# A grouped 1x1 convolution: TensorE in a loop over a 288-column input ring, a separate output ring, and a balancing piece for 15 DMA engines

## The chip, the cores and the metric

The kernel runs on one core of one Trainium2 chip. The metric is the device time in microseconds (us); the lower the better. All runs that are compared here were fast.

Names: PE is TensorE, PEld its weight loads, ACT is ScalarE, DVE is VectorE, POOL is GpSimd, SP is SyncE. Sixteen DMA engines move the data: SP issues the loads, ACT the stores.

## The reference, cut to what matters

```python
x: (1, 512, 512, 192) bf16        # 262,144 pixels of 192 channels
w: (1, 1, 4, 48, 48) bf16         # 4 groups of 48 channels, a 1x1 kernel
xg = x.reshape(1, 512, 512, 4, 48)
out = einsum('bhwgc,gcd->bhwgd', xg, w[0, 0])      # then back to (1, 512, 512, 192)
```

Each pixel is multiplied by a block-diagonal matrix. 100.7 MB are read and 100.7 MB written. In the kernel before, the DMA packets take 474 us of each DMA engine on average and the matmuls and transposes 431 us of PE, in a span of 483 us.

## The kernel before

Pixels are laid out as 128 rows by 2,048 columns, 384 bytes each. A *piece* of 104 columns is one load. Four columns are a *group*: PE transposes them (6 transposes), DVE copies a pair of groups out of PSUM, PE multiplies (6 matmuls), ACT copies the result out of PSUM. In the kernel before, ACT writes the result over the input, in the same ring, and the store leaves from there; a slot of the ring is loaded again when its store has landed. The lines below are cut and shortened; `wq.wait` waits for a semaphore.

```python
BIG = 104
RCOLS = 5 * BIG                      # one ring, 520 columns, for input and output
HEAD = (8, 20, 32)
NARROW = ((0, 16), (32, 16))         # 32 rows x 48 columns: the odd pixels, in the middle
...
        def _(sp):
            for p in pieces:
                for q in pieces:
                    if q.slot == p.slot - RCOLS // BIG:
                        wq.wait(st_sem[q.i], st_val[q])          # the store has landed
                for dram, sbuf in transfers(xf, ring, p):
                    sp.dma_start(sbuf, dram).then_inc(ld_sem[p.i], 16)
...
            for pair in range(NP):                               # PE, all written out
                if pair + 1 < NP:
                    transposes(pair + 1)
                matmuls(pair)
...
            for g in range(NG):                                  # ACT
                wq.wait(mm_done, g + 1)
                act.copy(dst_in_ring, o_ps[...]).then_inc(fa_done, 1)
                while todo and todo[0][3] <= g:
                    store()
```

## Time and profile before

| | before |
|---|---|
| time, median of 3 runs | 485.43 us (485.34 to 485.75) |
| span of the profile | 483.3 us |
| last PE instruction ends | 461.0 us |
| all DMA packets, summed, over 16 engines | 474.0 us |
| instruction-fetch packets | 50 |

The page of the kernel before. The first rows are busy times and the share of the span; then the busy tenths and the granted clock in 40 slices, then the DMA queues (q1 the loads, q10 the stores, q8 the instruction fetches) with packets, MB and their share of 16 engines' span; then the chain of waits that ended last, by engine.

```profile
PE 431.3 (89%) x6262; PEld 392.1 (81%) x6262; DVE 250.2 (52%) x262; ACT 392.6 (81%) x522; POOL 1.3 (0%) x8
...
PE   5699999999999999998599999979998999999910
...
PEclk9979999999999999999799999998999999999965
DMA  8999999999999999999999999999999999999993
...
q10 hardware_dynamic: 4360, 100.67, 48.7%
q1 hardware_dynamic: 3416, 100.68, 48.7%
q8 instruction: 50, 0.82, 0.6%
...
PE 54%; DMA 39%; ACT 1%; issue 1%; SPq 0%; ACTq 0%
```

The DMA row is full from the second slice to the last but one, while PE is done before the last slices. So the DMA engines hardly ever waited for compute here. The waits (who waited for whom: total us, times, longest) and the queue waits of SP say the same: PE's only sizeable waits are for loads, SP's are for stores to land.

```profile
ACT ring L260 <- PE o_ps L218: 61.0, 133, 7.9
PEld o_ps L218 <- ACT ring L260: 30.2, 126, 0.2
PE xT_ps L203 <- DMA ring<-in_x_dram: 21.1, 8, 6.8
```

```profile
SPq L175 <- DMA out_dram<-ring: 342.7, 15, 31.6
```

The windows view of the end (start:end, then busy us of each engine; the last three columns are granted clock, DMA share and GB/s) shows stores alone from 464 us on, until the last one lands:

```profile
452.00:464.00 12.00, 8.56 (x121) 7.24 (x118) 4.39 (x5) 9.23 (x13) 0.00 (x0) 0.95 1.00 424
464.00:476.00 12.00, 0.00 (x0) 0.00 (x0) 0.00 (x0) 0.00 (x0) 0.00 (x0) 0.50 0.81 343
476.00:488.00 12.00, 0.00 (x0) 0.00 (x0) 0.00 (x0) 0.00 (x0) 0.00 (x0) 0.61 0.09 37
```

The falling share in the last two rows is the DMA engines ending one after another. The trace's packet records do not name their engine, but on a busy engine each packet begins 3 or 4 ns before the recorded end of the one ahead of it, which lets them be chained into 16 engines. One of the 16 takes 1531 ns on average for a 39,936-byte packet for which most take 1476. It ends last, at 482.4 us. This document calls it the slow engine. The eight engines that carry instruction fetches (5 or 6 of the 50 packets each) are others.

### The profile page before, as it was taken

The page shows a single profiled execution, that of the slowest core. Times are in us where ns is not written, and L with a number is a line of the kernel's source. Part 1 is how long each engine was busy: PE and PEld are TensorE (multiplying, and loading weights), DVE is VectorE, ACT ScalarE, POOL GpSimd, SP SyncE. Part 2 cuts the span into 40 slices and gives each one's busy share as a digit, 9 for nine tenths or more (in the row PEclk, how much of TensorE's full clock was granted, in tenths as well). Part 3 has the DMA queues.
Part 4 walks back from the last instruction along what each step waited for, and adds up shares of the span by engine and source line. Part 5 has one row for each costly group of instructions (what it writes and reads, how often), then busy time and mean ns, then how long its engine had stood idle before and what let it go on. Part 6 is the DMA issues. An engine that isn't in the chain of part 4 may idle for free.

```text
span 483.3 us, 13933 instructions
## 1 busy us (share of the span) xinstructions
PE 431.3 (89%) x6262; PEld 392.1 (81%) x6262; DVE 250.2 (52%) x262; ACT 392.6 (81%) x522; POOL 1.3 (0%) x8
## 2 busy tenths in 40 slices
PE   5699999999999999998599999979998999999910
PEld 5599888898898889887588988969787898899800
DVE  2345655656555565564256555544554655556500
ACT  2669999999999999998299999877888999999920
POOL 1000000000000000000000000000000000000000
PEclk9979999999999999999799999998999999999965
DMA  8999999999999999999999999999999999999993
GB/s 351 431 406 421 449 425 421 422 424 442 434 428 419 425 420 439 425 434 424 431 434 437 424 431 428 432 431 426 434 428 428 430 424 422 439 416 427 429 390 156
DMA packets 7834, 202.23 MB, mean 418 GB/s; under 512 B 1056, under 2 KB 1056, under 8 KB 1696
## 3 DMA queue, kind: packets, MB, share of 16 engines
q10 hardware_dynamic: 4360, 100.67, 48.7%
q1 hardware_dynamic: 3416, 100.68, 48.7%
q8 instruction: 50, 0.82, 0.6%
q14 instruction: 8, 0.07, 0.0%
HBM read 100.68 MB, written 100.66 MB: 417 GB/s over the span
## 4 chain that ended last, share of the span: by engine, by line
PE 54%; DMA 39%; ACT 1%; issue 1%; SPq 0%; ACTq 0%
PE o_ps L218 31%; PE xT_ps L203 22%; DMA ring<-in_x_dram 20%; DMA out_dram<-ring 19%; ACT ring L260 1%; SPq L175 0%; ACTq L254 0%; SPq L169 0%
## 5 line engine op out<-in xcount | busy, mean ns | idle before, releaser
L260 ACT CAST ring<-o_ps 128x768 bf16<-128x768 f32 x521 | 391.3, 802 | 68.5 <-PE o_ps L218 61.0
L242 DVE COPY xT_sb<-xT_ps 128x1536 bf16<-128x1536 bf16 (+1 forms) x261 | 249.6, 956 | 206.0 <-PE xT_ps L203 206.0
L218 PE MATMUL o_ps<-wt,xT_sb 128*128 128x144 bf16 (+1 forms) x3126 | 292.0, 236 | 5.9 <-ACT ring L260 1.3
L218 PEld LDWEIGHTS o_ps<-wt,xT_sb 128*128 128x128 bf16 x3126 | 212.0, 99 | 43.4 <-ACT ring L260 30.2
L203 PE MATMUL xT_ps<-ident,ring 128*128 128x128 bf16 x3126 | 222.7, 221 | 21.1 <-DMA ring<-in_x_dram 21.1
L203 PEld LDWEIGHTS xT_ps<-ident,ring 128*128 128x128 bf16 x3126 | 191.1, 99 | 22.7 <-DMA ring<-in_x_dram 19.8
L188 PE MATMUL o_ps<-w_sb,esel 48*128 48x48 bf16 x10 | 0.6, 210 | 2.7 <-DMA w_sb<-in_w_dram 2.7
L188 PEld LDWEIGHTS o_ps<-w_sb,esel 48*128 48x128 bf16 x10 | 0.5, 113 | 2.6 <-POOL esel L158 2.6
L236 DVE CAST wt<-o_ps 128x480 bf16<-128x480 f32 x1 | 0.7, 658 | 3.3 <-PE o_ps L188 3.3
L260 ACT ACT_TABLE_LOAD x1 | 1.3, 1283 | 0.8 <-PEq L280 0.8
L158 POOL TENSOR_SCALAR_AFFINE_SELECT esel<-esel 48x272 bf16<-48x272 bf16 x1 | 0.4, 405 | 0.0
L155 POOL MEMSET esel<- 48x272 bf16 x1 | 0.3, 318 | 0.3 <-POOLq L280 0.3
L162 POOL TENSOR_SCALAR_AFFINE_SELECT ident<-ident 128x128 bf16<-128x128 bf16 x1 | 0.3, 285 | 0.0
L156 POOL MEMSET ident<- 128x128 bf16 x1 | 0.2, 198 | 0.0
L280 POOL MEMSET const-bfloat16-1.0<- 128x1 bf16 x1 | 0.1, 102 | 0.0
L280 POOL MEMSET const-uint8-127<- 128x1 uint8 x1 | 0.1, 102 | 0.0
L280 POOL MEMSET const-float32-0.0<- 128x1 f32 x1 | 0.1, 98 | 0.3 <-issue 0.3
L280 POOL MEMSET const-float32-1.0<- 128x1 f32 x1 | 0.1, 98 | 0.0
## 6 DMA issues: line engine op xcount, KB each, us to landing
ring<-in_x_dram SPq DMA_DIRECT2D x19, 4992.0 KB, 37.5
out_dram<-ring ACTq DMA_DIRECT2D x13, 4992.0 KB, 45.5
out_dram<-ring ACTq DMA_DIRECT2D x10, 2496.0 KB, 47.7
out_dram<-ring ACTq DMA_DIRECT2D x3, 1536.0 KB, 19.7
ring<-in_x_dram SPq DMA_DIRECT2D x1, 1536.0 KB, 8.4
out_dram<-ring ACTq DMA_DIRECT2D x1, 1152.0 KB, 16.6
ring<-in_x_dram SPq DMA_DIRECT2D x1, 960.0 KB, 5.2
out_dram<-ring ACTq DMA_DIRECT2D x1, 960.0 KB, 28.6
```

Of the source, the lines that this page charges most:

```text
L155: gp.memset(esel[:], 1.0).then_inc(p0_sem, 1)
L156: gp.memset(ident[:], 1.0).then_inc(p1_sem, 1)
L158: gp.affine_select(out=esel[:], in_=esel[:], pattern=[[-1, ECOLS]], compare_op=AluOpType.is_equal, fill=0.0, base=ESHIFT, channel_multipli ...
L162: gp.affine_select(out=ident[:], in_=ident[:], pattern=[[-1, 128]], compare_op=AluOpType.is_equal, fill=0.0, base=0, channel_multiplier=1) ...
L188: last = pe.matmul(o_ps[:, NOB - 1, col:col + CG], lhsT=esel[:, s0:s0 + 128], rhs=w_sb[:, g, :], start=True, stop=True, skip_group_check=True)
L203: last = pe.transpose(xT_ps[:, g % NXP, j * 128:(j + 1) * 128], xg[:, j * 128:(j + 1) * 128], ident[:])
L218: last = pe.matmul(o_ps[:, v % NOB, c0_:c1_], lhsT=xs[:, j * 128:(j + 1) * 128], rhs=wt[:, WOFF[tc]:WOFF[tc] + (c1_ - c0_)], start=(tc == ...
L236: dve.tensor_copy(wt[:], o_ps[:, NOB - 1, 0:WCOLS]).then_inc(wc_sem, 1)
L242: dve.tensor_copy(xT_sb[pair % NXS][:, 0:n * 2 * UC].rearrange("p (g c) -> p g c", g=n), xT_ps[:, b0:b0 + n, 0:2 * UC]).then_inc(e_done, 1)
L260: act.copy(dst, o_ps[:, v % NOB:v % NOB + 2, 0:UC]).then_inc(fa_done, 1)
L280: nc = _bacc.Bacc("TRN2", target_bir_lowering=False, num_devices=1)
```

## The change

The intent, as far as the code shows it: relieve the slow DMA engine of 64 columns, rid the others of most instruction fetches by letting PE run the same code six times, and free an input slot as soon as PE has transposed it, with a ring of its own for the output. The loop's body is written with fixed ring addresses, so it covers the input ring exactly once: 288 columns are 72 groups, 1,728 weight loads and matmuls.

```diff
-BIG = 104
-RCOLS = 5 * BIG
-HEAD = (8, 20, 32)
-NARROW = ((0, 16), (32, 16))
-NARROW_COLS = 48
+BIG = 96
+SLOTS = 3
+RCOLS = SLOTS * BIG
+OCOLS = 232
+HEAD = (8, 24, 64)
+PARTIAL = (
+    ("sync", 0, 16, 4), ("sync", 32, 16, 4),
+    ("pool", 52, 44, 11), ("pool", 20, 12, 3), ("pool", 96, 32, 8),
+)
+PARTIAL_COLS = 64
+PARTIAL_SLOT = 20
... in plan_pieces:
+    few = PARTIAL_COLS * sum(b[2] for b in PARTIAL)
+    partial = npix >= few + 128 * BIG * (PARTIAL_SLOT + 1)
... SP: a slot is free when it has been transposed
+                if freed(p) > seen:
+                    seen = freed(p)
+                    sp.wait_ge(t_done, seen)
... PE: counters are taken down again, so that the code can be repeated
+                            if j == 2 and g >= 2:
+                                last.then_inc(fa_done[(g - 2) % (2 * NTOK)], -1)
...
-            for pair in range(NP):
-                if pair + 1 < NP:
-                    transposes(pair + 1)
-                matmuls(pair)
+            first = LA // 2 if LR > 1 else NP
+            for pair in range(first):
+                step(pair)
+            if LR > 1:
+                with pe.Fori(0, LR):
+                    for pair in range(first, first + LB // 2):
+                        step(pair)
+                for pair in range(first + LR * LB // 2, NP):
+                    step(pair)
... ACT: before it writes to the out ring, the store that held those columns must have landed
+                if over[g] is not None:
+                    landed(over[g])
+                act.copy(out_columns(g)..., o_ps[...]).then_inc(fa_done[...], 1)
... gpsimd issues its share of the 64-column piece (cut)
```

More of the change, by code (lines that the diff above doesn't have):

```diff
@@ L23 @@
 ECOLS = 272
-BIG = 104
-RCOLS = 5 * BIG
-HEAD = (8, 20, 32)
-LATE = 6
-LATE_PARTS = (52, 52)
-LAST_PARTS = (32, 32, 24, 16)
-FULL = ((0, 128),)
-NARROW = ((0, 16), (32, 16))
-NARROW_COLS = 48
-NARROW_AT = (9,)
+BIG = 96
[3 more added lines that the diff above has]
+HEAD = (8, 24, 64)
+LATE_COLS = 240
+LATE_PART = 48
+LAST_PARTS = (24, 20, 16, 8)
 NXP = 4
@@ L37 @@
 NOB = 4
-class Waiter:
-    def __init__(self, eng):
-        self.eng = eng
-        self.seen = {}
-    def wait(self, sem, val):
-        if val <= 0 or self.seen.get(sem.num, 0) >= val:
-            return
-        self.seen[sem.num] = val
-        self.eng.wait_ge(sem, val)
+NTOK = 6
+FULL = (("sync", 0, 128, 128),)
+PARTIAL = (
[4 more added lines that the diff above has]
+PARTIAL_SLOT = 20
+FILL_ROWS = 5
+FILL_BEFORE = (2, 3)
 class Piece:
@@ L59, in __init__ @@
         self.blocks = []
-        for (r0, rows) in blocks:
-            self.blocks.append((r0, rows, pix))
+        for (queue, r0, rows, outer) in blocks:
+            self.blocks.append((queue, r0, rows, outer, pix))
             pix += rows * size
@@ L64, in __init__ @@
         assert size % 4 == 0 and self.at + size <= RCOLS
+class Store:
+    def __init__(self, piece, c0, c1, at):
+        self.piece, self.c0, self.c1, self.at = piece, c0, c1, at
+        self.g0, self.g1 = piece.g0 + c0 // 4, piece.g0 + c1 // 4
 def plan_pieces(npix):
-    few = NARROW_COLS * sum(rows for _, rows in NARROW)
-    at = [i for i in NARROW_AT if npix >= len(NARROW_AT) * few + 128 * (sum(HEAD) + BIG * (i + 2))]
-    cols = (npix - few * len(at)) // 128
+    few = PARTIAL_COLS * sum(b[2] for b in PARTIAL)
+    partial = npix >= few + 128 * BIG * (PARTIAL_SLOT + 1)
+    cols = (npix - few * partial) // 128
     assert cols % 4 == 0
-    head = list(HEAD) if cols >= sum(HEAD) + BIG else []
+    head = list(HEAD) if cols >= sum(HEAD) else []
     mid = cols - sum(head)
     slots = [[(BIG, FULL)]] * (mid // BIG) + ([[(mid % BIG, FULL)]] if mid % BIG else [])
-    for i in at:
-        slots.insert(i, [(NARROW_COLS, NARROW)])
     if head:
         slots.insert(0, [(s, FULL) for s in head])
+    if partial:
+        slots.insert(PARTIAL_SLOT, [(PARTIAL_COLS, PARTIAL)])
     pieces, g, pix = [], 0, 0
     for n, parts in enumerate(slots):
-        c = n * BIG % RCOLS
+        c = n % SLOTS * BIG
         for s, blocks in parts:
@@ L86, in plan_pieces, with plan_stores, loop_span @@
     return pieces
+def plan_stores(pieces):
+    total = sum(p.size for p in pieces)
+    stores, at = [], 0
+    for p in pieces:
+        after = total - 4 * p.g1
+        if p is pieces[-1] and sum(LAST_PARTS) == p.size:
+            parts = list(LAST_PARTS)
+        elif after < LATE_COLS and p.full and p.size > LATE_PART:
+            parts = [LATE_PART] * (p.size // LATE_PART) + ([p.size % LATE_PART] if p.size % LATE_PART else [])
+        else:
+            parts = [p.size]
+        c = 0
+        for n in parts:
+            if not p.full and at + n > OCOLS:
+                at = 0
+            while n:
+                m = min(n, OCOLS - at)
+                stores.append(Store(p, c, c + m, at))
+                c, n, at = c + m, n - m, (at + m) % OCOLS
+    return stores
+def loop_span(pieces, ng):
+    body = RCOLS // 4
+    a = next((p.g0 for p in pieces if p.slot == 1), ng)
+    b = a
+    for p in pieces:
+        if p.slot >= 1 and p.g0 == b and p.full and p.size == BIG:
+            b = p.g1
+    rounds = max(0, (b - a - 2) // body)
+    return a, body, rounds
 def bass_standalone__grouped__vision_kernel(nc, x, w, out):
@@ L95, in bass_standalone__grouped__vision_kernel @@
     pieces = plan_pieces(npix)
+    stores = plan_stores(pieces)
     piece_of = {g: p for p in pieces for g in range(p.g0, p.g1)}
+    store_of = {g: s for s in stores for g in range(s.g0, s.g1)}
     NG = pieces[-1].g1
     NP = (NG + 1) // 2
+    LA, LB, LR = loop_span(pieces, NG)
+    assert LA % 2 == 0 and LB % (2 * NXS) == 0 and LB % (2 * NTOK) == 0 and LB % NXP == 0
     xf = x.rearrange("b h w c -> (b h w) c")
@@ L105, in groups, with transfers @@
         return range(2 * pair, min(2 * pair + 2, NG))
-    def transfers(ap, ring, p, c0=0, c1=None):
-        c1 = c1 or p.size
-        for (r0, rows, pix) in p.blocks:
+    def transfers(ap, tile, at, p, c0, c1, queues):
+        for n, (queue, r0, rows, outer, pix) in enumerate(p.blocks):
+            if queue not in queues:
+                continue
             px = ap[pix:pix + rows * p.size, :]
@@ L113, in transfers @@
             else:
-                view = px.rearrange("(c a i) n -> a c (i n)", a=4, c=rows // 4)
-            yield view, ring[r0:r0 + rows, (p.at + c0) * C:(p.at + c1) * C]
-    stores = []
+                assert (c0, c1) == (0, p.size)
+                view = px.rearrange("(c a i) n -> a c (i n)", a=outer, c=rows // outer)
+            yield n, view, tile[r0:r0 + rows, at * C:(at + c1 - c0) * C]
+    ld_key = {}
     for p in pieces:
-        late = pieces[-1].slot - p.slot
-        parts = LAST_PARTS if late == 0 else LATE_PARTS if late < LATE else (BIG,)
-        c = 0
-        for n in parts if p.size == BIG and p.full else (p.size,):
-            stores.append((p, c, c + n, p.g0 + (c + n) // 4))
-            c += n
-    st_val = {p: 16 * sum(len(p.blocks) for q, *_ in stores if q is p) for p in pieces}
+        part = sum(1 for q in pieces if q.slot == p.slot and q.i < p.i)
+        for n in range(len(p.blocks)):
+            ld_key[p.i, n] = (p.slot % SLOTS, part) if p.full else ("partial", n)
+    partial = [p for p in pieces if not p.full]
     with ExitStack() as es:
@@ L129, in bass_standalone__grouped__vision_kernel @@
         ring = es.enter_context(nc.sbuf_tensor("ring", [128, RCOLS * C], BF16))
+        oring = es.enter_context(nc.sbuf_tensor("oring", [128, OCOLS * C], BF16))
         xT_sb = [es.enter_context(nc.sbuf_tensor(f"xT_sb{i}", [128, 4 * UC], BF16)) for i in range(NXS)]
@@ L134, in bass_standalone__grouped__vision_kernel @@
         wt = es.enter_context(nc.sbuf_tensor("wt", [128, WCOLS], BF16))
+        fill = es.enter_context(nc.sbuf_tensor("fill", [FILL_ROWS, 32], BF16))
         xT_ps = es.enter_context(nc.psum_tensor("xT_ps", [128, NXP, 1024], BF16))
@@ L139, in sem @@
             return es.enter_context(nc.semaphore(name))
-        ld_sem = [sem(f"ld{p.i}") for p in pieces]
-        st_sem = [sem(f"st{p.i}") for p in pieces]
+        ld_sem = {k: sem("ld_" + "_".join(map(str, k))) for k in sorted(set(ld_key.values()), key=str)}
+        st_sem = [[sem(f"st{i}_{n}") for n in range(len(s.piece.blocks))] for i, s in enumerate(stores)]
         w_sem, id_sem, e_sem, wb_sem, wc_sem = (sem(s) for s in ("w_sem", "id_sem", "e_sem", "wb_sem", "wc_sem"))
@@ L145, in bass_standalone__grouped__vision_kernel @@
         t_done, mm_done = sem("t_done"), sem("mm_done")
-        e_done, fa_done = sem("e_done"), sem("fa_done")
+        e_done = [sem(f"e_done{i}") for i in range(NTOK)]
+        fa_done = [sem(f"fa_done{i}") for i in range(2 * NTOK)]
+        fin = sem("fin")
+        go_sem = sem("go_sem")
+        fill_sem = [sem(f"fill{i}") for i in range(2 * len(FILL_BEFORE))]
         def columns(g):
@@ L151, in columns, with out_columns, freed @@
             return ring[:, at * C:(at + 4) * C]
+        def out_columns(g):
+            s = store_of[g]
+            at = s.at + 4 * (g - s.g0)
+            return oring[:, at * C:(at + 4) * C]
+        def freed(p):
+            last = [q for q in pieces if q.slot == p.slot - SLOTS]
+            return last[-1].g1 // 2 if last else 0
         @block.gpsimd
@@ L164, in _, with filler @@
                              channel_multiplier=1).then_inc(id_sem, 1)
+            fills = list(fill_sem)
+            for p in partial:
+                def filler(n):
+                    if n in FILL_BEFORE:
+                        k = len(fill_sem) - len(fills)
+                        src = xf[0:2 * FILL_ROWS, 0:4].rearrange("(p t) n -> p t n", t=2)
+                        dst = fill[:, 8 * k:8 * k + 8].rearrange("p (t n) -> p t n", t=2)
+                        gp.dma_start(dst, src).then_inc(fills.pop(0), 16)
+                gp.wait_ge(t_done, freed(p))
+                for n, dram, sbuf in transfers(xf, ring, p.at, p, 0, p.size, ("pool",)):
+                    filler(n)
+                    gp.dma_start(sbuf, dram).then_inc(ld_sem[ld_key[p.i, n]], 16)
+                gp.wait_ge(go_sem, 1)
+                for i, s in enumerate(stores):
+                    if s.piece is p:
+                        for n, dram, sbuf in transfers(of, oring, s.at, p, s.c0, s.c1, ("pool",)):
+                            filler(n)
+                            gp.dma_start(dram, sbuf).then_inc(st_sem[i][n], 16)
+            for k, s in enumerate(fill_sem):
+                if k < len(fill_sem) - len(fills):
+                    gp.wait_ge(s, 16)
         @block.sync
         def _(sp):
-            wq = Waiter(sp)
             sp.dma_start(w_sb[:], wv).then_inc(w_sem, 16)
+            seen = 0
             for p in pieces:
-                for q in pieces:
-                    if q.slot == p.slot - RCOLS // BIG:
-                        wq.wait(st_sem[q.i], st_val[q])
-                for dram, sbuf in transfers(xf, ring, p):
-                    sp.dma_start(sbuf, dram).then_inc(ld_sem[p.i], 16)
+                if freed(p) > seen:
+                    seen = freed(p)
+                    sp.wait_ge(t_done, seen)
+                for n, dram, sbuf in transfers(xf, ring, p.at, p, 0, p.size, ("sync",)):
+                    sp.dma_start(sbuf, dram).then_inc(ld_sem[ld_key[p.i, n]], 16)
         @block.tensor
         def _(pe):
-            wq = Waiter(pe)
             def build_weights():
-                wq.wait(e_sem, 1)
-                wq.wait(w_sem, 16)
+                pe.wait_ge(e_sem, 1)
+                pe.wait_ge(w_sem, 16)
                 last = None
@@ L192, in transposes @@
             def transposes(pair):
-                wq.wait(e_done, pair - 1)
-                last = None
+                todo = []
                 for g in groups(pair):
                     p = piece_of[g]
+                    if g % 2 and pair:
+                        pe.wait_ge(e_done[(pair - 1) % NTOK], 1)
                     if g == p.g0:
-                        wq.wait(ld_sem[p.i], 16 * len(p.blocks))
+                        keys = [ld_key[p.i, n] for n in range(len(p.blocks))]
+                        for key in keys:
+                            pe.wait_ge(ld_sem[key], 16)
+                        todo += keys if p.full else []
                     xg = columns(g)
@@ L204, in transposes @@
                                                 xg[:, j * 128:(j + 1) * 128], ident[:])
+                            if todo and 0 < j < 5:
+                                last.then_inc(ld_sem[todo.pop(0)], -16)
+                assert not todo
                 last.then_inc(t_done, 1)
             def matmuls(pair):
-                wq.wait(e_done, pair + 1)
+                if pair + 1 == NP or len(groups(pair + 1)) < 2:
+                    pe.wait_ge(e_done[pair % NTOK], 1)
                 for g in groups(pair):
                     xs = xT_sb[pair % NXS][:, g % 2 * 2 * UC:(g % 2 + 1) * 2 * UC]
-                    wq.wait(fa_done, g - 1)
+                    if g >= 2:
+                        pe.wait_ge(fa_done[(g - 2) % (2 * NTOK)], 1)
                     last = None
@@ L220, in matmuls, with step @@
                                              start=(tc == 0), stop=(tc == 2), skip_group_check=True)
+                            if j == 2 and g >= 2:
+                                last.then_inc(fa_done[(g - 2) % (2 * NTOK)], -1)
+                            if j == 1 and g % 2 == 0:
+                                last.then_inc(e_done[pair % NTOK], -1)
                     last.then_inc(mm_done, 1)
-            build_weights()
-            wq.wait(id_sem, 1)
-            transposes(0)
-            wq.wait(wc_sem, 1)
-            for pair in range(NP):
+            def step(pair):
                 if pair + 1 < NP:
@@ L230, in _ @@
                 matmuls(pair)
+            build_weights()
+            pe.wait_ge(id_sem, 1)
+            transposes(0)
+            pe.wait_ge(wc_sem, 1)
+            first = LA // 2 if LR > 1 else NP
[7 more added lines that the diff above has]
+                    step(pair)
         @block.vector
         def _(dve):
-            wq = Waiter(dve)
-            wq.wait(wb_sem, 1)
+            dve.wait_ge(wb_sem, 1)
             dve.tensor_copy(wt[:], o_ps[:, NOB - 1, 0:WCOLS]).then_inc(wc_sem, 1)
@@ L239, in _ @@
                 b0 = pair * 2 % NXP
-                wq.wait(t_done, pair + 1)
-                wq.wait(mm_done, 2 * (pair - NXS + 1))
+                dve.wait_ge(t_done, pair + 1)
+                if pair >= NXS:
+                    dve.wait_ge(mm_done, 2 * (pair - NXS + 1))
                 dve.tensor_copy(xT_sb[pair % NXS][:, 0:n * 2 * UC].rearrange("p (g c) -> p g c", g=n),
-                                xT_ps[:, b0:b0 + n, 0:2 * UC]).then_inc(e_done, 1)
+                                xT_ps[:, b0:b0 + n, 0:2 * UC]).then_inc(e_done[pair % NTOK], 1)
@@ L245, in _, with landed @@
         @block.scalar
         def _(act):
-            wq = Waiter(act)
-            todo = list(stores)
-            def store():
-                p, c0, c1, g1 = todo.pop(0)
-                wq.wait(fa_done, g1)
-                for dram, sbuf in transfers(of, ring, p, c0, c1):
-                    act.dma_start(dram, sbuf).then_inc(st_sem[p.i], 16)
-            for g in range(NG):
-                wq.wait(mm_done, g + 1)
+            done = set()
+            def landed(i):
+                if i not in done:
+                    done.add(i)
+                    for one in st_sem[i]:
+                        act.wait_ge(one, 16)
@@ new lines, in _, with issue @@
+            todo = list(range(len(stores)))
+            def issue(i):
+                s = stores[i]
+                for n, dram, sbuf in transfers(of, oring, s.at, s.piece, s.c0, s.c1, ("sync",)):
+                    act.dma_start(dram, sbuf).then_inc(st_sem[i][n], 16)
+                if any(b[0] == "pool" for b in s.piece.blocks):
+                    act.sem_inc(go_sem, 1)
+            over = {}
+            for i, s in enumerate(stores):
+                for c in range(s.at, s.at + s.c1 - s.c0, 4):
+                    g = s.g0 + (c - s.at) // 4
+                    before = [k for k in range(i) if stores[k].at <= c < stores[k].at + stores[k].c1 - stores[k].c0]
+                    over[g] = before[-1] if before else None
@@ L258, in _ @@
+            for g in range(NG):
+                act.wait_ge(mm_done, g + 1)
+                while todo and stores[todo[0]].g1 <= g - 1:
+                    issue(todo.pop(0))
+                if over[g] is not None:
+                    landed(over[g])
                 v = 2 * g
-                dst = columns(g).rearrange("p (u c) -> p u c", u=2)
-                act.copy(dst, o_ps[:, v % NOB:v % NOB + 2, 0:UC]).then_inc(fa_done, 1)
-                while todo and todo[0][3] <= g:
-                    store()
+                act.copy(out_columns(g).rearrange("p (u c) -> p u c", u=2),
+                         o_ps[:, v % NOB:v % NOB + 2, 0:UC]).then_inc(fa_done[g % (2 * NTOK)] if g < NG - 2 else fin, 1)
@@ L263, in _ @@
+            act.wait_ge(fin, min(2, NG))
             while todo:
-                store()
-            for p in pieces:
-                wq.wait(st_sem[p.i], st_val[p])
+                issue(todo.pop(0))
+            for i in range(len(stores)):
+                landed(i)
 _INS = ['x', 'w']
```

## The prediction

> **What bounds the kernel now.** The DMA engines. The windows view shows a DMA share of 0.99 to 1.01 and 423 to 430 GB/s in every stretch from 10 to 460 us; PE is busy 431 us of 483.3, and the timeline shows PE and ACT pacing each other at 3.27 us per four groups (about 0.82 us a group, 418 us for 512), so compute has over 10% to spare. In the last 20 us stores alone drain.
>
> It is one DMA engine, not the mean of 16. The trace's packet records chain exactly (each starts 3 ns before the last one of its engine ends), which separates the engines up to 388 us: most move a 39,936-byte packet in 1476 ns (median), one needs 1531 ns on average (loads 1493, stores 1581). Eight engines each carry 5 or 6 of the 50 instruction fetches (16,384 bytes, 977 ns); the slow engine carries none. Four others carry the narrow piece (16 packets of 686 ns, 11 us). From where the last packets end: three engines stop near 466 us, the fetching ones near 475, the narrow ones 475 to 480, the slow one at 482.4, which is the end. Shared evenly, the packets would take 474 us.
>
> **The change.** (a) PE loops six times over 72 groups (1,728 loads and matmuls). [...] If the body stays resident, fetches fall from 50 to about 15; if not, they stay near 50 with six short PE stalls. Either way it relieves engines that are not last: 0 on the critical path. (b) The input slot is freed by the transposes, not the store, but room shrinks from 520 shared columns to 288 in and 232 out. (c) The 64-column piece is meant to take 393 KB (about 14.5 us) off the slow engine. But its condition asks for 7,680 + 128·96·21 = 265,728 pixels and there are 262,144. The built program has no DMA on gpsimd, and loads 8, 24, 64, twenty of 96, and 32 columns. **So the piece is not there**, and neither is the old narrow piece: every engine now moves 2,048 columns, the slow one 12 more than before.
>
> **Cost.** Slow engine: 480 us for 2,036 columns, times 2048/2036 = +2.8 us. Tail: ACT now waits for out-ring room and the last store is 32 columns (1,536 KB, 3.7 us) rather than 16; stores no longer lie 20 us deep behind PE. I estimate 3 to 5 us in which the DMA engines wait for PE at the end, and 0 to 3 us elsewhere, because the slow engine's backlog shrinks.  Span about 489.5; the runs are 2.1 us longer than the profile's span: 491.5 us, range 487 to 498. Faster by over 2%: 0.03; within: 0.79; slower: 0.18.
>
> **What would show it.** Fetch packets on the instruction queue near 15; no POOL-queue packets; loads of 4,608 KB x20; DMA share near 1.0 until about 460 us, then a ragged end; one engine with slow packets finishing last; "ACT waits for DMA out_dram" as a new wait, SP waiting for PE instead of stores.
>
> **What would make it wrong.** If the slow engine's extra time came from the instruction stream, the loop would remove it and the time would fall to about 475. If the jump back stalls PE by more than about 5 us, or the 232-column out ring starves the DMA engines each piece, it would be 500 or more.

The sum is a span of 483.3 us, +2.8 for the slow engine, 0 for the loop and 3.4 out of the 3 to 8 estimated for the waits, which makes about 489.5, and about 2 from the span to the run, 491.5. That the stops would be short, and the limit of 5 us for a jump, were guesses with no trace behind them. The "about 15" fetches are an estimate from the page of the kernel before: 50 packets for 12,524 loads and matmuls are one for 250, and of the 12,308 of the changed kernel 3,668 remain if five of the six rounds need no fetch.

## The result

| | before | after |
|---|---|---|
| time, median of 4 runs each | 485.38 us | 507.47 us (505.72 to 509.46) |
| ratio of the fast runs | | 1.0456 (95%: 1.0426 to 1.0486) |
| span of the profile | 483.3 us | 504.0 us |
| last PE instruction ends | 461.0 us | 497.4 us |
| all DMA packets over 16 engines | 474.0 us | 485.7 us |
| instruction-fetch packets | 50 | 59 |

A ratio is the mean time of one kernel's fast runs over that of the kernel before in the same rounds, so it is not quite the ratio of the medians. The change costs 22 us; the predicted loss was 6, and the range ended at 498.

The same parts of the page after:

```profile
PE 432.9 (86%) x6154; PEld 393.8 (78%) x6154; DVE 245.9 (49%) x257; ACT 388.2 (77%) x513; POOL 1.3 (0%) x8
...
PE   5999995759999389999399996699993899999994
...
PEclk9999998879999789999689999799996999999998
DMA  8999999999999999999986999999999989999967
...
q1 hardware_dynamic: 3664, 100.68, 48.7%
q10 hardware_dynamic: 5040, 100.67, 47.0%
q8 instruction: 59, 0.97, 0.7%
...
PE 70%; ACT 10%; issue 10%; DMA 8%; ACTq 0%; SPq 0%
```

PE is as busy as before in us, but has notches at regular distances, down to 3, and runs into the last slice. The chain that ended last has turned from DMA (39% to 8%) to PE, with 10% "issue", which is time in which an engine waited for nothing that the profile shows. In order of time, the long "issue" pieces of that chain (start us, us, what) are these:

```profile
98.06 6.55 issue
...
167.96 7.85 issue
...
238.68 7.95 issue
...
311.04 6.50 issue
...
380.03 7.74 issue
```

Five pieces, about 71 us apart: the five jumps back of a loop of six rounds. PE's own branch records stand at the same places and last 6.96, 8.27, 8.33, 6.92 and 8.16 us, while the last, which falls through, lasts 0.08 us. A second, shorter stop of 1.06 to 1.84 us follows each, 10 to 13 us after the first began. The waits view has the two kinds of stop as "issue"; together they are 43.9 us (36.6 + 7.3):

```profile
PE xT_ps L288 <- issue: 36.6, 5, 8.0
...
PE o_ps L308 <- issue: 7.3, 5, 1.8
```

A stop costs more than its length. The trace's clock records show half the clock for 6.8 to 13.7 us, beginning 2.4 to 4.5 us after each jump began. When PE works again, 12 transposes take 1.28 to 1.46 us, against 0.83 us at the full clock. Until PE's last instruction, 54.6 us of the changed kernel ran at half clock and 17.1 us of the kernel before.

The fetches have not fallen to 15 but risen to 59: the loop body is fetched again in every round (nine packets from the end of one long jump to the end of the next). The queue waits of SP, which were for stores, are now for PE:

```profile
SPq L257 <- PE xT_ps L288: 438.4, 19, 32.4
```

The end shows what bounds now. PE works at full rate to 497 us while the DMA share falls to 0.82 and 0.61:

```profile
464.00:476.00 12.00, 11.76 (x180) 10.81 (x178) 6.82 (x8) 10.84 (x15) 0.00 (x0) 1.00 1.00 422
476.00:488.00 12.00, 11.73 (x177) 10.65 (x177) 6.70 (x7) 11.06 (x16) 0.00 (x0) 1.00 0.82 344
488.00:500.00 12.00, 8.56 (x122) 7.36 (x119) 4.79 (x5) 9.42 (x13) 0.00 (x0) 1.00 0.61 258
```

One trap of reading: the DMA share is still 0.98 to 1.01 in most stretches of the middle. Part of this is stretched packets: loads of 36,864 bytes took 1436 ns on average, with a median of 1364, and many of the long ones (means of 1.8 to 2.1 us) stand in the first 8 us of five loads that were issued 4.5 to 9.3 us after the load before had landed. Each of these five comes 27 to 31 us after a jump began: here PE's stops reach the DMA engines, because a late PE frees its input slots late. A full DMA row does not say that the DMA engines set the pace; who runs on at the end does.

### The profile page after: what moved, and what is told of

It reads as the page before. It is cut to its first block, busy times and chain, and to the rows that moved or that the text cites. A ratio compares the mean times of both kernels' runs of the same rounds, so it can differ in the third digit from the quotient of the medians.

```text
span 504.0 us, 13475 instructions
## 1 busy us (share of the span) xinstructions
PE 432.9 (86%) x6154; PEld 393.8 (78%) x6154; DVE 245.9 (49%) x257; ACT 388.2 (77%) x513; POOL 1.3 (0%) x8
## 2 busy tenths in 40 slices
DMA packets 8772, 202.39 MB, mean 402 GB/s; under 512 B 1152, under 2 KB 1152, under 8 KB 1920
## 4 chain that ended last, share of the span: by engine, by line
PE 70%; ACT 10%; issue 10%; DMA 8%; ACTq 0%; SPq 0%
PE o_ps L308 41%; PE xT_ps L288 30%; ACT oring L383 10%; DMA out_dram<-oring 7%; DMA ring<-in_x_dram 1%; ACTq L364 0%; SPq L257 0%; SPq L250 0%; ACTq L357 0%
## 5 line engine op out<-in xcount | busy, mean ns | idle before, releaser
L383 ACT CAST oring<-o_ps 128x768 bf16<-128x768 f32 x512 | 386.9, 801 | 109.2 <-PE o_ps L308 95.3
L346 DVE COPY xT_sb<-xT_ps 128x1536 bf16<-128x1536 bf16 x256 | 245.2, 958 | 246.4 <-PE xT_ps L288 246.4
L308 PEld LDWEIGHTS o_ps<-wt,xT_sb 128*128 128x128 bf16 x3072 | 215.2, 100 | 57.3 <-ACT oring L383 40.1
L288 PE MATMUL xT_ps<-ident,ring 128*128 128x128 bf16 x3072 | 224.7, 225 | 39.8 <-issue 36.6
```

The lines of the kernel that those rows point to most:

```text
L288: last = pe.transpose(xT_ps[:, g % NXP, j * 128:(j + 1) * 128], xg[:, j * 128:(j + 1) * 128], ident[:])
L308: last = pe.matmul(o_ps[:, v % NOB, c0_:c1_], lhsT=xs[:, j * 128:(j + 1) * 128], rhs=wt[:, WOFF[tc]:WOFF[tc] + (c1_ - c0_)], start=(tc == ...
L346: dve.tensor_copy(xT_sb[pair % NXS][:, 0:n * 2 * UC].rearrange("p (g c) -> p g c", g=n), xT_ps[:, b0:b0 + n, 0:2 * UC]).then_inc(e_done[pa ...
L383: act.copy(out_columns(g).rearrange("p (u c) -> p u c", u=2), o_ps[:, v % NOB:v % NOB + 2, 0:UC]).then_inc(fa_done[g % (2 * NTOK)] if g < ...
```

## The experiments

Two theories at the start. **Jump theory**: the loss is PE standing still at jumps. **Ring theory**: 288 and 232 columns are too few, and ACT or the loads starve for room whatever PE does. A third, **balance theory**: without any narrow piece the slow DMA engine has more to do, and the missing 64-column piece is what costs. Fourteen kernels ran in four sets; each set shared one chip.

### Loop written out

`unrolled`: the changed kernel, all of PE's work written out.

```diff
-            first = LA // 2 if LR > 1 else NP
+            first = NP
-            if LR > 1:
+            if False:
```

> The changed kernel with PE's loop written out (no jump back), everything else the same. Jump theory: the loss is PE standing still about 9 us at each of five jumps back; without them PE has no gap over 0.5 us after the first 10 us except waits for out-ring room, fetch packets fall from 59 to about 50, and the time falls to 487 to 495 us, DMA-bound again. Small-ring theory: the 288-column input ring and 232-column out ring starve the DMA engines whatever PE does; the time stays at 500 us or more.

Measured: 496.41 us (495.49 to 499.47), ratio 1.0233 (1.0210 to 1.0256). 48 fetches, no "issue" stop. This is between the two theories: taking away the jumps gives back about 11 of the 22 us, not all, and both expectations miss. The waits show why 43.9 us of stops are worth only 11. The unrolled kernel:

```profile
PE o_ps L308 <- ACT oring L383: 43.3, 40, 8.8
ACT oring L383 <- DMA out_dram<-oring: 41.6, 10, 9.3
```

The changed kernel:

```profile
PE o_ps L308 <- ACT oring L383: 10.9, 28, 5.5
...
ACT oring L383 <- DMA out_dram<-oring: 5.9, 1, 5.9
```

Without jumps, ACT stands 41.6 us waiting for stores to land before it may overwrite the out ring, and PE stands behind ACT. With jumps, PE comes late and most of the room is already free. The jumps replaced that wait and then went beyond it: PE's gaps of over 0.7 us after the first 12 us sum to 49.5 us with jumps and 37.0 us without, a difference of 12.5 us that is close to the 11 us. So both theories hold in part, one behind the other. Half the clock followed these waits too (41.0 us in `unrolled`).

### The piece switched on

`loop_piece`: the changed kernel with the piece's condition mended. `unrolled_piece`: the same without the loop.

```diff
-    partial = npix >= few + 128 * BIG * (PARTIAL_SLOT + 1)
+    partial = npix >= few + 128 * BIG * PARTIAL_SLOT
```

> The changed kernel with the condition of the 64-column piece mended (times PARTIAL_SLOT instead of PARTIAL_SLOT + 1), so that the piece is really moved, on 15 DMA engines; loop kept. Jump theory: PE is the bound and has one group more to do, so nothing is gained: 503 to 510 us. Balance theory (the loss is that no piece relieves the slow DMA engine): the time falls to 485 to 492 us.

> Both: loop written out and piece on. Jump theory plus slow-engine account: with PE out of the way the slow DMA engine is the bound again, and 60 columns less on it than on the others (about 14 us) count: 477 to 484 us, below before. If the gpsimd transfers skip the wrong engine, or their overhead costs as much: 488 to 495 us, no better than the unrolled kernel without the piece.

Measured: `loop_piece` 511.86 us (median of the three fast runs), ratio 1.053 (1.051 to 1.0551); `unrolled_piece` 499.78 us (498.09 to 500.16), ratio 1.0291 (1.0277 to 1.0305). Each is slower than its partner without the piece (`loop_piece` and the changed kernel, 1.0456, ran in different sets and are compared by their ratios). The balance theory falls. The second result also missed my own expectation (477 to 484). It is not that the wrong engine was spared: chaining the packets from 405 to 460 us, the one engine with slow stores (1.08 times the usual) carries none of the piece's 24,576-byte packets beyond two that the chaining probably misplaced, and the others about eight. The tiny filler DMAs of the change (four of 0.1 KB, issued by gpsimd) seem meant to steer the piece past the slow engine. The trace shows that the piece misses it; no run without the fillers shows that they are the reason. In these rings the DMA engines are not the bound: in `unrolled_piece` PE ends at 490.3 us and all sixteen engines 4 to 7 us later, so relieving one of them buys nothing. Why the piece makes the kernel slower is not shown.

### What a jump consists of

`short_packets`: the changed kernel, loop kept, each larger load and store cut into two DMAs of alternate column blocks, so that no data packet exceeds 9,216 bytes.

```diff
-            yield n, view, tile[r0:r0 + rows, at * C:(at + c1 - c0) * C]
+            view = view.rearrange("p (k f) -> p k f", k=k)      # k = 2 or 4
+            to = to.rearrange("p (k f) -> p k f", k=k)
+            for h in range(2):
+                yield n, view[:, h::2, :], to[:, h::2, :]
... loads and stores so cut are waited for with 32 instead of 16 (cut)
```

> The changed kernel, loop kept, with each load and store of over 24 columns cut into two transfers of alternate column blocks, so that a DMA packet is at most 9,216 bytes (350 ns) instead of 36,864 (1364 ns). If an instruction fetch after a jump waits behind data packets on its DMA engine, the jump shrinks from 7 to 8.3 us to 3 to 5 us and the later gap of 1 to 1.8 us nearly vanishes, and the time falls to 487 to 498 us. If the jump has a fixed cost of its own, it stays at 7 to 8 us and the time at 503 to 510 us.

Measured: 511.97 us, ratio 1.056 (1.0541 to 1.058); the jumps last 6.07 to 6.93 us (mean 6.31 against 7.73). Shorter, but far less than expected, and the time is no better; the doubled DMA issues were not separated from the rest.

`probe`: the unrolled kernel with six extra loops on PE ahead of the work, of four rounds each, that only transpose the identity. The DMA engines are idle for most of the loops (the DMA row of its page is 0 in 19 of the 40 slices).

```diff
             build_weights()
             pe.wait_ge(id_sem, 1)
+            pe.wait_ge(ld_sem[1, 0], 16)
+            for n in (64, 104, 200, 360, 488, 840):
+                with pe.Fori(0, 4):
+                    for k in range(n):
+                        pe.transpose(xT_ps[:, k % NXP, 0:128], ident[:], ident[:])
             transposes(0)
```

> The unrolled changed kernel with six extra loops on PE ahead of the work, four rounds each, of 64, 104, 200, 360, 488 and 840 transposes (twice as many instructions: 128, 208, 400, 720, 976, 1680) of the identity; the results stay right. The DMA engines are idle for most of it, so a jump's cost is seen without other traffic. [...] If a jump costs about 6 us even with idle DMA engines, the cost is its own; if 2 to 4 us, the rest was waiting behind data packets.

Two alternatives: by the one, the jumps over 720 instructions and more would each cost several us; by the other, all six would be cheap.

Measured: jumps back over 128, 208, 400, 720 and 976 instructions last 0.21 to 0.23 us, stop PE nowhere, and after the first round the body is not fetched again. Jumps back over 1,680 instructions last 3.95, 3.33 and 3.86 us, and the body is fetched in every round, nine packets at a time. Neither of the two alternatives came true. Nor do 3.3 to 4.0 us with idle DMA engines show that the rest of a jump was waiting behind data packets, as the expectation would conclude; the fetches are looked at below. The timeline across the last jump of the 976-instruction loop, at 271.30 us, then across the first of the 1,680-instruction loop, at 345.45 us (the second with the idle time in brackets):

```profile
269.79 3.40 PE L328 MATMUL xT_ps<-ident 128*128 128x128 bf16 x58
```

```profile
344.32 2.17 PE L328 MATMUL xT_ps<-ident 128*128 128x128 bf16 x36
...
349.46 0.84 PE L328 MATMUL xT_ps<-ident 128*128 128x128 bf16 x12 [2.96 <-issue]
```

The fetch packets in the traces take a long jump apart. In every long jump of three kernels, the branch record ends 2.3 to 2.4 us after the start of the last fetch packet before it. What varies is the time from the branch to that packet's start:

| | wait for the fetch packet to start | from its start to the end of the jump |
|---|---|---|
| probe, idle DMA engines | 0.98 to 1.63 us | 2.3 to 2.4 us |
| short_packets | 3.68 to 4.60 us | 2.3 to 2.4 us |
| changed kernel | 4.58 to 5.99 us | 2.3 to 2.4 us |

So about half of a jump's cost in the changed kernel (4.0 of 7.7 us) is that the fetch starts later than with idle DMA engines. Part of that seems to be data in the way: shorter packets went with a wait that is 1.4 us shorter on average. On average the wait was 5.4 us with long packets and 4.0 with short ones, against 1.4 with idle engines, so 4.0 and 2.6 us more. The longest data packets take 1364 ns in the one kernel (36,864 bytes) and about 350 ns in the other (estimated from the 347 ns of the 9,216-byte stores of the changed kernel), so the extra wait is as long as about 3 packets in the one and about 7 in the other (estimates from these times). A wait for a fixed number of data packets does not explain both. In what order a DMA engine takes fetches and data packets is not shown. Another candidate stands in the traces and was not tested. In the changed kernel another fetch packet starts between 0.8 us before and 0.7 us after each branch begins, in `short_packets` 0.5 to 1.4 us before, in the probe 2.7 to 2.9 us before. If the fetch for the jump has to wait until that one is done (2.3 to 2.4 us after its start, if it takes as long as the last one does), it can start late however short the data packets are. It stays open which it is.

### The terms of the prediction one by one

`before_even`: the kernel before without its narrow piece, so that every engine moves 2,048 columns.

```diff
-    at = [i for i in NARROW_AT if npix >= ...]
+    at = [i for i in () if npix >= ...]
```

> The kernel before without its narrow piece: every DMA engine moves 2,048 columns, as in the changed kernel, but with the shared 520-column ring and no loop. Slow-engine account: the slow engine gets 12 columns more, +2.8 us, so 487 to 490 us; this is the prediction's first term by itself. If the narrow piece does nothing: 485.4 us.

Measured: 487.27 us (487.10 to 488.00), ratio 1.004 (1.0027 to 1.0053), that is +1.9 us (0.004 times 485.2). One engine's packets end at 485.3 us, the next one's at 480.0. The slow-engine account fits; the term was estimated at 2.8, just above the interval (1.3 to 2.6 us).

`out328`: the unrolled changed kernel with the same 520 columns divided 192 in, 328 out. The pieces shrink from 96 to 64 columns with it; the loop is written out as in `unrolled`, and the 64-column piece is held off (`partial = False`).

```diff
-BIG = 96
-OCOLS = 232
-HEAD = (8, 24, 64)
+BIG = 64
+OCOLS = 328
+HEAD = (8, 24, 32)
```

> The changed kernel, loop written out, with the same 520 columns divided otherwise: input ring 192 (three slots of 64), out ring 328. Out-ring theory (what keeps the unrolled kernel 11 us above before is ACT waiting for out-ring room, 40 us of PE gaps): these gaps shrink below 15 us and the time falls to 486 to 491 us. If it is the split itself (two rings cannot lend room to each other): the waits move to loads and the time stays at 493 us or more.

Measured: 489.29 us (489.19 to 489.45), ratio 1.0083 (1.0070 to 1.0096). The time is as the out-ring theory said. The gaps are not: PE still has 22.5 us of gaps over 0.7 us behind ACT, and ACT's wait for landed stores is 26.2 us rather than the 41.6 of `unrolled`. Those that remain hardly matter, because PE ends at 465 us, 21 us ahead of the last packet; in `unrolled` it ended at 487 us, 7 us ahead. The same wait is harmless in one kernel and costly in the other, and the end tells which.

`before_piece`: the kernel before with its narrow piece replaced by the 64-column piece, in the middle.

```diff
-NARROW = ((0, 16), (32, 16))
-NARROW_COLS = 48
+NARROW = (("sync", 0, 16, 4), ("sync", 32, 16, 4),
+          ("pool", 52, 44, 11), ("pool", 20, 12, 3), ("pool", 96, 32, 8))
+NARROW_COLS = 64
...
+ gpsimd issues the "pool" blocks, with semaphores of their own, as the change does (cut)
... the last, shorter piece is stored in parts of 24, 16 and 16 columns (cut)
```

> The kernel before with its narrow piece replaced by the change's 64-column piece on 120 rows (15 engines, partly by gpsimd), in the same place in the middle; shared 520-column ring, no loop. Slow-engine account: the slow engine moves 1,988 columns instead of 2,036, the fetching engines 2,052 become last at about 476 us, so 477 to 481 us. If the gpsimd transfers cost what they save, or a deep ring was not what the piece lacked: 484 us or more.

Measured: 483.61 us (483.22 to 486.74), ratio 0.9985 (0.9962 to 1.0007): not clear of noise, and short of the 477 to 481 expected. The packets, summed, are 476.3 us per engine against 474.0, and PE waits 16.3 us once for a load of this piece. The engines now end between 475 and 481 us, but the fetches are still there (49), and the piece stands in the middle.

### A loop that stays at hand, with a deep out ring

`ring144`: input ring 144 columns (three slots of 48), out ring 376, loop body 36 groups (864 weight loads and matmuls). `ring144_unrolled`: the same without the loop. `ring192`: the rings of `out328` with the loop, body 1,152. `ring144_piece`: `ring144` with the piece on, as two pieces of 32 columns near the end. In the other three the piece is held off (`partial = False`).

```diff
-BIG = 96
-OCOLS = 232
-HEAD = (8, 24, 64)
+BIG = 48
+OCOLS = 376
+HEAD = (8, 16, 24)
... ring144_piece only:
-PARTIAL_COLS = 64
-PARTIAL_SLOT = 20
+PARTIAL_COLS = 32
+PARTIAL_SLOT = 35
+PARTIALS = 2
-    partial = npix >= few + 128 * BIG * (PARTIAL_SLOT + 1)
+    partial = npix >= few + 128 * BIG * PARTIAL_SLOT
```

> The changed kernel with the loop kept but its body shortened: input ring 144 columns (three slots of 48), loop body 36 groups (864 loads and matmuls, between the 976 instructions that stayed at hand in the probe and far below 1,728), 13 rounds; out ring 376 of the same 520 columns; no piece. Residency account: each of the 12 jumps costs about 0.2 us, the fetch packets fall from 48 to about 10, no PE gap stands at a jump, and the time is that of an unrolled kernel with a large out ring, 486 to 490 us. If a loop costs PE several us a jump whatever its body: 12 times 8 us more, above 510 us.

> The same rings as ring144 (144 in, 376 out), loop written out. Against ring144 it shows what a loop that stays at hand is worth: the fetch packets (about 48 of 0.95 us on eight of the engines that are not the slow one) cost nothing where the slow engine bounds, so within 1 us of ring144, 486 to 490 us. If the fetches do count: 2 to 4 us above ring144.

> The rings of out328 (192 in, three slots of 64; 328 out) with the loop kept: body 48 groups, 1,152 loads and matmuls, 10 rounds. The probe left open whether a body between 976 and 1,680 instructions stays at hand. If it does: fetches near 15, jumps 0.2 us, 488 to 491 us as out328. If not: nine jumps of 7 to 8 us, fetches near 60, and since PE has about 25 us of waits to give up, 510 to 535 us.

> ring144 (loop at hand, out ring 376) with the piece on, as two pieces of 32 columns on 120 rows near the end. If a deep out ring is what the piece needs, the slow DMA engine is 60 columns lighter than the rest and the eight fetching engines carry almost no fetches: 476 to 482 us, below before. If the gpsimd transfers cost as much as they save, as the run on the kernel before suggests (1.6 us gained of 6): 483 to 487 us.

Measured:

| kernel | time, us | ratio (95%) | fetches |
|---|---|---|---|
| ring144 | 488.83 | 1.0064 (1.0050 to 1.0078) | 7 |
| ring144_unrolled | 488.51 | 1.0063 (1.0049 to 1.0077) | 48 |
| ring192 | 491.28 | 1.0122 (1.0107 to 1.0138) | 7 |
| ring144_piece | 479.32 | 0.9870 (0.9855 to 0.9885) | 14 |

The instruction queue of `ring144`, where the changed kernel had 59 packets:

```profile
q8 instruction: 7, 0.11, 0.1%
```

All twelve jumps of `ring144` and all nine of `ring192` last 0.21 to 0.24 us. So a body of 1,152 loads and matmuls still stays at hand; between there and the probe's 1,680 lies the limit. `ring192` came out a little above its range (491.28 against 488 to 491). Without the piece the loop is worth nothing: `ring144` and `ring144_unrolled` agree, although one has 41 fetches fewer. With the piece, the kernel is faster than both the kernel before (by 1.3%, clear of noise) and the changed one.

The last set separates the loop from the piece, on one chip. `r144_piece_again` is `ring144_piece` unchanged; `r144_piece_unrolled` differs in this:

```diff
-            first = LA // 2 if LR > 1 else NP
+            first = NP
-            if LR > 1:
+            if False:
```

> ring144_piece once more, as the partner of the next run on the same chip: 479 to 481 us again.

> ring144_piece with the loop written out. If fetches matter once the slow DMA engine is relieved: about 34 fetch packets of 0.95 us come back, on eight engines (4 us each), which are then the last ones: 482 to 485 us, 3 to 5 us above its partner. If the piece alone made the gain: within 1 us of its partner.

Measured: `r144_piece_again` 479.09 us, ratio 0.9878 (0.9863 to 0.9892); `r144_piece_unrolled` 485.10 us, ratio 1.0009 (0.9973 to 1.0044). In these rings, then, as ratios to the kernel before:

| | no piece | piece |
|---|---|---|
| loop written out | 1.0063 | 1.0009 |
| loop at hand | 1.0064 | 0.9878 |

The loop alone gives nothing, the piece alone about half a per cent, both together 1.8%; the two columns come from two sets and are compared by ratio.

The packets of the last 60 us, chained into engines, show which end last. In `ring144` one engine ends at 486.7 us and the other fifteen between 470.4 and 475.5. In `ring144_unrolled` one ends at 485.9, eight more at 478.4 to 479.1, the rest by 474.1. So without the piece the slow engine decides, with the fetches or without them. With the piece, all sixteen end together: at 474.7 to 476.1 us in `r144_piece_again` (PE at 468.5), at 482.1 to 482.8 in `r144_piece_unrolled` (PE at 476.0). The expectation for the latter came close in number (485.10 against 482 to 485) and had the path wrong: no eight engines run on at the end, but PE is 7.5 us late, after longer waits for loads. First the kernel written out, then the one with the loop:

```profile
PE xT_ps L290 <- DMA ring<-in_x_dram: 33.4, 19, 12.2
```

```profile
PE xT_ps L290 <- DMA ring<-in_x_dram: 25.5, 19, 8.5
```

That the fetches are what delays these loads is argued from the one thing that differs, the loop; the traces were not followed further.

The page of `r144_piece_again`:

```profile
DMA  8999999999999999999999999999999999999997
...
q0 software_dynamic: 1216, 4.33, 2.3%
q8 instruction: 14, 0.23, 0.2%
```

The DMA row is full up to the last slice, where before it stood at 3: the engines now end closer together. (q0 is the gpsimd share of the piece.)

## Why the prediction was wrong

**Wrong step 1: "if not, they stay near 50 with six short PE stalls. Either way it relieves engines that are not last: 0 on the critical path."** I counted on a loop of 1,728 loads and matmuls that stays at hand, or else on stops that cost nothing; both were assumptions that no trace showed. The stops were five, not short (6.9 to 8.3 us, and 1.1 to 1.8 us more a little later, 43.9 us in all), and they were on the critical path (10% of the chain that ended last is "issue"): PE had about 22 us between its last instruction and the end of the kernel before. The rings alone left 7 of these (`unrolled`), so the loop found no room and costs 11 us net (507.5 against 496.4). The text did name the right danger, "if the jump back stalls PE by more than about 5 us ... 500 or more", but gave it too little weight. The step "off the bounding engine, so zero" fails when the cost lands on another engine than the gain: the gain was on DMA engines with room to spare, the cost on PE.

**Wrong step 2: "3 to 5 us in which the DMA engines wait for PE at the end, and 0 to 3 us elsewhere".** The separate rings, with the pieces of 96 columns and the other store sizes that came with them, cost 9.1 us (`unrolled` 496.4 less `before_even` 487.3), against 3 to 8 estimated: the term was mis-sized by little, and part of its path was wrong. The out ring of 232 columns made ACT wait 41.6 us for stores, PE fell behind, and the last input could only be worked off after the loads had ended at 453 us: PE ended at 487. Dividing the same columns as 192 and 328 brought back 7 us. That run also has smaller pieces, but `ring144_unrolled`, with smaller ones still and 376 columns out, is as good; I take the room in the out ring to be the cause.

**Right in kind: the slow engine's 12 more columns.** Predicted +2.8 us, measured +1.9.

**Right: the piece is not there.** The page has no gpsimd queue, and the loads are twenty of 4,608 KB. Switching it on in the changed kernel makes it slower still; it paid clearly only in `ring144_piece`, where the DMA engines are the bound and the loop stays at hand; in `before_piece`, where they are the bound too, it gained nothing clear of noise.

The sum: 485.4 before, +1.9 for the columns, +9.1 for the rings, +11.1 for the loop gives 507.5, the measured time. That is a breakdown and no check: each term is the difference of two kernels in a row, so the sum must close, and another order of the steps could give other terms. The three terms come from different sets of runs, each beside its own runs of the kernel before (485.2 to 485.4).

**Of the signs that I had named**, these came: no gpsimd queue, loads of 4,608 KB, SP waiting for PE, a ragged end, and a wait of ACT for the out ring (5.9 us; 41.6 without the loop). These did not: fetches near 15 (59), and a slow DMA engine that ends last (PE did).

## What to carry to other kernels

Before a loop is put on an engine to save instruction fetches, check what a jump back costs, by a loop of the intended length, and whether the engine that pays for the jump has that time to give; here a body of up to 1,152 instructions was free (jumps of 0.21 to 0.24 us), and one of 1,680 or more was fetched every round and stopped the engine each time (jumps of 3.3 to 8.3 us). When one buffer is split in two, each part can no longer lend room to the other, so look at which wait is new and at which engine runs on at the end, not at busy shares. A balancing measure can pay only while its resource is the bound, so measure it together with the changes that make it so: here loop and piece together gave 1.8% where the one alone gave nothing and the other half a per cent.
